# Re-placing the second half of batch 1 in a one-core attention and MLP kernel

## The chip, the cores and the metric

The kernel runs on one core of a Trainium2 chip. The core has a matrix engine (TensorE, PE in the profile; its weight loads are listed apart as PEld), a vector engine (VectorE, DVE), a scalar engine (ScalarE, ACT), a general engine (GpSimd, POOL) and a queue that issues DMAs (SyncE, SP). Each works through its own instructions in order, and they wait for each other through semaphores. Matmul results go into PSUM banks, from which VectorE and ScalarE copy them out.

The metric is the device time of one execution in microseconds (us). Before the change it is 303.61 us, the median of three runs (303.59 to 303.66).

## The reference

For 8 batches of 576 tokens with 8 heads of 64 channels, causal attention in a window of 64 tokens, and then a normalised two-layer MLP with a residual:

```python
scores = scale * np.matmul(q, k.transpose(0, 1, 3, 2))
mask = (rel >= 0) & (rel < window)          # rel = query position - key position, window = 64
attn = softmax(np.where(mask, scores, -1e9))
x = np.matmul(attn, v)                      # heads side by side: 8 x 576 x 512
xn = (x - mu) / np.sqrt(var + 1e-06) * g_ln # mean and variance over the 512 channels
out = x + np.maximum(xn @ w_ch1, 0.0) @ w_ch2   # 512 -> 2048 -> 512
```

## The kernel before

**Tiling.** The first 512 tokens of a batch are one group of work, and the last 64 tokens of all eight batches make a ninth group. A group has four blocks of 128 tokens (0 to 3; `kb`, `j` in the code). A batch goes through these steps, each a helper function:

- `load_qk`, `load_v` issue DMAs on SP; `cast_qk`, `cast_v` cast to 16 bit on GpSimd. A batch's Q and K come in two halves.
- `t_main(b, x, half)` transposes half of Q (`x=0`) or K (`x=1`) with eight TensorE transposes into a PSUM tile (L267), and `evac` copies that into `qkT` on ScalarE or VectorE (L248, L250). For the pairs in `PAIRED` (L277) the tile is half of the two-bank tile `xps`, else a bank from `t_tile`.
- `s_pe(b, j)` computes the scores of a block: 16 matmuls (L340) into two banks, which are `sc`, `xps` or `t0` and `t1` (`home`). `s_exp` exponentiates them on ScalarE into `pt` (two instructions, L350), `s_mask` multiplies with the mask on VectorE (L360).
- `b_pe(b, kb)` multiplies with V (16 matmuls, two for each head; L387). A 65th column of ones gives the row sums, and `b_rows` divides by them on VectorE, takes mean and variance (L403 to L412) and in batches 0 and 1 also computes the centred rows `z` (L423; for block 0 of batch 1 on ScalarE, L427).
- `zt_step` transposes `z` of a block with four transposes (L456) into a `t_tile` bank, and ScalarE (L459) or VectorE (L461) copies them into `zT`.
- The MLP of a group is a list of units (`mlp_units`). In group 0 these are 8 units of half width (`l1_half`, L621) and 8 of full width for the first layer, then ten units `l2_three` (numbers 16 to 25), which compute the second layer for token blocks 0, 1 and 2, each one unit behind the one before (L638), and four units that compute it for block 3 (26 to 29, four matmuls each, L491). In group 1 the first eight units use tokens 0 to 255 (so `zT` of blocks 0 and 1), the next eight tokens 256 to 511, and a ScalarE relu takes each result out of its bank (L626). `add_out(kb)` adds a block's second-layer result, its "output column" below, to the rows on VectorE (L501) and stores it.

**Order.** There is no planner. `at(i, f, ...)` puts a call behind unit `i` of the current group, and at the end the units are run in order, each followed by its calls. The order of these calls is the order of the instructions on every engine. While group `g` runs its MLP, the slots bring the next batch through attention: in group 0 the steps of batch 1, in group 1 the rest of batch 1 and those of batch 2.

**PSUM.** The eight banks are two `sc`, the two of `xps`, `t0` and `t1`, and two `mm`. `t_tile` takes `t0` and `t1` in turn, or `t0` alone while `tbank["shared"]` is set: from unit 17 of group 0 on, `t1` holds the second-layer sum of block 2 and is given back by `add_out(2)`. The sums of blocks 0 and 1 are in the two `mm` banks, which the sum of block 3 and the first unit of group 1 take over in turn. A step that uses a bank waits until its last reader is done. GpSimd's queue holds a one-element copy that waits for the mask of block 3 (`after_mask`, L353), and behind it the casts of the rest of Q and K of batch 2.

Of the kernel before, what the change touches and what calls it, by code (L numbers as in the profile page):

```python
# [18 lines left out]
def kernel(  # L19
# [17 lines left out]
    NHC = HID // 128  # L37
# [32 lines left out]
    tbank = {"n": 0, "shared": False}  # L70

    def t_tile(shape, name):
        i = 0 if tbank["shared"] else tbank["n"] % 2
        tbank["n"] = i + 1
        return ps_t.tile(shape, FP16, tag=f"t{i}", name=name)
# [167 lines left out]
    def flat(b):  # L243
        return qkT[b][0][:, :, :].rearrange("p h m -> p (h m)")

    def evac(x, out, in_):
        if x == 0:
            nc.scalar.copy(out=out, in_=in_)  # L248
        else:
            nc.vector.tensor_copy(out=out, in_=in_)  # L250

    def t_main(b, x, half, eng=None):
        src = qk16.pop((b, x, half))
        if b >= XQ and x == 0:
            dst = flat(b)[:, 2 * SM * half:2 * SM * half + 2 * SM]
            nc.sync.dma_start_transpose(out=dst.rearrange("p (a t) -> p a t", t=128),
                                        in_=src[:, :].rearrange("p a e d -> p (a e d)"))
            return
        j = 2 if b < 2 else 4
        if (b, half) in PAIRED:  # L260
            if x == 0:
                both_tp[b] = ps_x.tile([128, 2, 8, 128], FP16, tag="xps", name=f"tp_{b}_{half}")
            tp = both_tp[b][:, x]
        else:
            tp = t_tile([128, 8, 128], f"tp_{b}_{x}_{half}")
        for i in range(8):
            nc.tensor.transpose(out=tp[:, i, :], in_=src[:, i], identity=ident16)  # L267
        if b < 2:
            c0 = 64 * x + 256 * half
            dst = qkT[b][x][:, :, c0:c0 + 256]  # L270
        else:
            dst = qkT[b][x][:, 2 * half:2 * half + 2, 64 * x:64 * x + 512]
        evac(x if eng is None else eng, dst.rearrange("c h (p j) -> c h p j", j=j),
             (tp if (b, half) in PAIRED else tp[:, :]).rearrange("c (h j) p -> c h p j", j=j))

    both_tp = {}
    PAIRED = ((1, 1), (2, 0))  # L277

    def t_tail(i, x):
        src = tail16[i][x]  # L280
# [189 lines left out]
    def mlp_units(g, split=0, three=False, seven=True):  # L470
# [27 lines left out]
        def add_out(kb):  # L498
            xv = x_norm[(g, kb // 2)][:, kb % 2, :]
            if g < 2:  # L500
                nc.vector.scalar_tensor_tensor(  # L501
                    out=xv, in0=ch[kb], scalar=rstd[g][:, kb:kb + 1], in1=xv, op0=ALU.mult, op1=ALU.add,
                )
            else:
                nc.vector.tensor_tensor(out=xv, in0=ch[kb], in1=xv, op=ALU.add)
            store(kb)
# [122 lines left out]
        def l2_three(i):  # L629
            for kb in range(3):  # L630
                e = i - kb
                if e == 0 and kb == 2:
                    ch[kb] = ps_t.tile([128, DM], FP32, tag="t1", name=f"ch_{g}_{kb}")
                elif e == 0:
                    ch[kb] = ps_mm.tile([128, DM], FP32, tag="mm", name=f"ch_{g}_{kb}")
                if 0 <= e < NHC // 2:
                    for hc in (2 * e, 2 * e + 1):
                        nc.tensor.matmul(  # L638
                            out=ch[kb], lhsT=hrT[:, hc, 128 * kb:128 * (kb + 1)], rhs=w2s[:, hc, :],
                            start=(hc == 0), stop=(hc == NHC - 1),  # L640
                        )
                if e == NHC // 2 - 1:
                    add_out(kb)
                    if kb == 2:
                        tbank["shared"] = False
                        tbank["n"] = 0

# [117 lines left out]
        if three:  # L765
            for i in range(NHC // 2 + 2):
                units.append(lambda i=i: l2_three(i))
# [114 lines left out]
    for i in range(8):  # L882
        w1_cast(i, (0,) if i in (1, 3) else (0, 1))
    t_main(0, 0, 1, 0)
    keep_clock(1)
    b_step(0, 1)
    t_main(0, 1, 1, 0)
    zt_step(0, 0, "dve")
    keep_clock(2)
# [43 lines left out]
    for g in range(NGRP):  # L933
# [7 lines left out]
        def at(i, f, *a):  # L941
            slots[min(i, len(slots) - 1)].append((f, a))

        def first_scores(b, i):
            at(i, s_pe, b, 0)
            at(i, s_pe, b, 1, False, "xps")
            at(i, s_exp, b, 0, 0, 1)
            at(i + 1, s_exp, b, 1, 0, 1)
            at(i + 1, s_mask, b, 0)
            at(i + 2, s_mask, b, 1)  # L950

        b = g + 1
        if g == 0:
            at(0, w1_cast, 3, (1,), True)
            at(0, queue_up)
            at(1, zt_step, 0, 2, "dve")
            at(2, zt_step, 0, 3, "dve")
            at(11, t_main, 1, 0, 0, 1)
            at(12, t_main, 1, 1, 0, 1)
            at(16, s_pe, 1, 0)  # L960
            at(16, s_pe, 1, 1, False, "xps")
            at(16, s_exp, 1, 0, 0, 1)
            at(16, s_mask, 1, 0)
            at(17, s_exp, 1, 1, 0, 1)
            at(17, s_mask, 1, 1)
            for c in range(2):
                at(20, vB_cur, 1, c, 0)
                at(20, vB_prev, 1, c, 0)
            at(22, b_pe, 1, 0)
            at(22, b_pe, 1, 1, "sc")  # L970
            at(22, b_rows, 1, 0)
            at(22, z_step, 1, 0)
            at(23, b_rows, 1, 1)
            at(25, zt_step, 1, 0)
            at(26, t_main, 1, 0, 1, 0)
            at(27, t_main, 1, 1, 1, 0)
            at(27, lambda: tbank.update(n=0))
            at(28, zt_step, 1, 1, "dve")
            at(28, s_pe, 1, 2)
            at(28, s_pe, 1, 3, False, "t")  # L980
            at(28, s_exp, 1, 2, 0, 1)
            at(28, s_exp, 1, 3, 0, 1)
            at(29, s_mask, 1, 2)
            at(29, s_mask, 1, 3)
        if g == 1:
            at(0, cast_qk, 2, 0, (0,))
            at(0, after_mask, 1, 3)
            at(0, cast_qk, 2, 0, (1,))
            at(0, cast_qk, 2, 1)
            at(0, alloc_v, 2)  # L990
            at(0, alloc_qkT, 2)
            for c in (0, 2):
                at(0, cast_v, 2, c, c + 2)
                at(5, part_vB, 2, c)
            at(1, t_main, 2, 0, 0)
            at(2, b_pe, 1, 2, "t")
            at(2, b_pe, 1, 3, "sc")
            at(2, b_rows, 1, 2)
            at(2, b_rows, 1, 3)
            at(2, root, 1)  # L1000
            at(4, t_main, 2, 1, 0)
            at(5, zt_step, 1, 2)
            at(5, t_main, 2, 0, 1)
            at(7, zt_step, 1, 3)
            at(7, t_main, 2, 1, 1)
            at(7, w2_sums, 3, 0, 4)
            at(8, w2_sums, 3, 4, 8)
            at(25, w2_sums, 2, 0, 4)
            at(28, w2_sums, 2, 4, 8)
            at(9, s_pe, 2, 0)  # L1010
            at(9, s_pe, 2, 1, False, "xps")
            at(9, s_exp, 2, 0, 0, 1)
            at(10, s_mask, 2, 0)
            at(11, s_exp, 2, 1, 0)
            at(12, s_exp, 2, 1, 1)
            at(13, s_mask, 2, 1)
            for j in range(4):
                i = (14, 17, 20, 22)[j]
                if j < 3:
                    at(i, b_pe, 2, j)  # L1020
                if j < 2:
                    at(i, s_mm, 2, j + 2)
                    at(i + 1, s_mask, 2, j + 2)
                if j == 2:
                    at(i, b_pe, 2, 3, "sc")
                at(i, b_rows, 2, j)
                at(i, z_step, 2, j)
                at((18, 21, 24, 26)[j], z_act, 2, j)
                at((18, 21, 24, 26)[j], zt_step, 2, j)
            at(6, load_qk, 3, 0)  # L1030
            at(8, load_qk, 3, 1)
            at(10, load_v, 3, 0, 4)
            at(8, alloc_qkT, 3)
            at(8, cast_qk, 3, 0)
            at(14, cast_qk, 3, 1, (0,))
            at(17, cast_qk, 3, 1, (1,))
            at(22, alloc_v, 3)
            at(22, cast_v, 3, 0, 2)
            at(22, cast_v, 3, 2, 4)
            at(27, part_vB, 3, 0, 4)  # L1040
            first_scores(3, 30)
            for i, (x, half) in zip((12, 24, 18, 28), ((0, 0), (1, 0), (0, 1), (1, 1))):
                at(i, t_main, 3, x, half, 0)
            at(40, load_qk, 4, 0)
            at(40, load_qk, 4, 1)
            at(40, load_v, 4, 0, 2)
# [58 lines left out]
        n = g + 2  # L1105
# [75 lines left out]
```

## Time and profile before

| what | value |
|---|---|
| median of 3 runs | 303.61 us |
| the profiled execution | 303.57 us, span 301.2 us |
| TensorE busy | 291.5 us (97% of the span), mean granted clock 0.994 |
| VectorE, GpSimd, ScalarE busy | 208.3, 159.3, 154.2 us |
| first-layer matmuls L479 | 416 of 128x512, 94.7 us |
| half-width first-layer matmuls L621 | 192 of 128x256, 23.2 us |
| second-layer matmuls L638 and L491 | 48 and 80 of 128x512 |
| score exponentials L350 on ScalarE | 72, mean 600 ns |
| masks L360 on VectorE | 32, mean 740 ns |
| casts of Q and K L145 on GpSimd | 30, mean 1152 ns |

The span runs from the first to the last instruction. A row of the profile in order of time gives the start of a run of equal instructions in us from the start of the span, the time from its first start to its last end, the engine, the line of the kernel, the operation, output and inputs, shape and count; in brackets stands how long the engine was idle before it and what ended that. Matmuls overlap in TensorE's pipeline, so the duration of a row reaches into the next one. The change touches work between 44 and 67 us of the span.

### The profile page before, as it was taken

Reading aid. Unit: us, or ns where it says so; the run is one execution under the profiler, and the core shown is the slowest. Engines: PE = TensorE matmul, PEld = TensorE weight load, DVE = VectorE, ACT = ScalarE, POOL = GpSimd, SP = SyncE. Lnnn points to the kernel's source line nnn. Section 1 sums busy time; section 2 is a strip of 40 time slices with the busy share of each in tenths; the row PEclk is TensorE's granted clock in tenths of the full one; section 3 lists DMA queues with packets and bytes.
Section 4 is the critical chain, followed back from the end, with each engine's and each line's share of the span. In section 5 each row is a group of like instructions: output and inputs, shape, how many; then the busy total and the mean of one; then the engine's idle time right before and its main releaser. Section 6 shows DMA issues by size and latency. Waiting matters only on the chain.

```text
span 301.2 us, 7565 instructions
## 1 busy us (share of the span) xinstructions
PE 291.5 (97%) x3067; PEld 195.3 (65%) x3067; DVE 208.3 (69%) x409; ACT 154.2 (51%) x259; POOL 159.3 (53%) x234
## 2 busy tenths in 40 slices
PE   7989999999999999999999999999999999999992
PEld 3657545787554488557854786469646854788881
DVE  2771348584837986479767866698667775879972
ACT  4576644777458634873176428751664056206400
POOL 4688877634632886189608860897048307115200
PEclk9999999999999999999999999999999999999997
DMA  8999999989977999999299999991729396013014
GB/s 190 261 383 340 384 286 290 249 266 307 139 203 245 211 182 146 272 280 163 58 286 277 193 169 284 274 162 39 220 64 164 70 216 156 15 32 127 0 38 104
DMA packets 114020, 58.34 MB, mean 194 GB/s; under 512 B 83649, under 2 KB 104705, under 8 KB 113986
## 3 DMA queue, kind: packets, MB, share of 16 engines
q1 hardware_dynamic: 113696, 57.47, 80.4%
q8 instruction: 24, 0.39, 0.6%
q10 hardware_dynamic: 290, 0.40, 0.5%
q14 instruction: 10, 0.08, 0.1%
HBM read 38.80 MB, written 9.44 MB: 160 GB/s over the span
## 4 chain that ended last, share of the span: by engine, by line
PE 83%; DMA 8%; ACT 2%; POOL 2%; SPq 2%; issue 0%; DVE 0%; POOLq 0%
PE hps L479 28%; PE pA L556 12%; PE pB L556 8%; PE pC L556 8%; DMA qk<-in_k_dram 6%; PE ch L491 6%; PE hph L621 4%; PE xps L387 4%; PE sc L340 3%; PE lA L676 2%; DMA v<-in_v_dram 2%; PE tp L267 2%; PE lC L676 1%; POOL w2s L234 1%; SPq L167 1%; PE ch L638 1%
## 5 line engine op out<-in xcount | busy, mean ns | idle before, releaser
L479 PE MATMUL hps<-zT,w1g 128*128 128x512 f16 x416 | 94.7, 379 | 0.0
L483 ACT ACTIVATE hrT<-hps 128x512 f16<-128x512 f32 x104 | 62.3, 599 | 41.2 <-PE hps L479 37.8
L479 PEld LDWEIGHTS <-w1g 128*128 128x128 f16 x416 | 39.2, 98 | 45.4 <-issue 2.2
L350 ACT ACTIVATE pt<-sc 128x512 f16<-128x512 f32 x72 | 39.3, 600 | 21.4 <-PE sc L340 20.7
L556 PEld LDWEIGHTS <-sS 128*128 128x128 f16 x448 | 43.3, 98 | 4.9
L431 POOL TENSOR_SCALAR rsz<-mvg 128x1 f32<-128x1 f32 x28 | 9.7, 347 | 68.5 <-DVE mvg L412 66.5
L145 POOL CAST qk<-qk 128x1024 f16<-128x1024 f32 x30 | 34.0, 1152 | 8.4 <-DMA qk<-in_q_dram 4.9
L360 DVE TENSOR_TENSOR pt<-pt,mask 128x1024 f16<-128x1024 f16 x32 | 23.4, 740 | 20.6 <-ACT pt L350 20.6
L556 PEld LDWEIGHTS <-hrT 128*128 128x128 f16 x336 | 32.1, 98 | 6.4 <-ACT hrT L483 1.0
L248 ACT COPY qkT<-tp 128x1024 f16<-128x1024 f16 (+1 forms) x18 | 17.4, 966 | 25.2 <-PE tp L267 24.3
L556 PE MATMUL pC<-w2s,sS 128*128 128x256 f16 x224 | 26.9, 273 | 0.0
L556 PE MATMUL pA<-wT,sS 128*128 128x256 f16 x224 | 26.9, 273 | 0.0
L407 DVE TENSOR_TENSOR xn<-xps,rcp 128x256 f32<-128x256 f32 (+1 forms) x50 | 25.8, 539 | 0.9
L409 DVE BATCH_NORM_STATS2 stats<-xn 128x6 f32<-128x512 f32 x36 | 25.0, 695 | 1.2
L530 DVE TENSOR_TENSOR sS<-hrT 128x512 f16<-128x512 f16 (+1 forms) x40 | 24.3, 606 | 2.1 <-ACT hrT L483 2.0
L621 PE MATMUL hph<-zT,w1g 128*128 128x256 f16 x192 | 23.2, 273 | 0.6 <-ACT zT L459 0.5
L437 POOL TENSOR_SCALAR z<-xn,rsz 128x512 f16<-128x512 f32 x24 | 21.5, 898 | 2.5
L403 DVE RECIPROCAL rcp<-xps 128x4 f32<-128x4 f32 (+1 forms) x50 | 8.0, 181 | 19.7 <-PE xps L387 19.6
L621 PEld LDWEIGHTS <-w1g 128*128 128x128 f16 x192 | 18.1, 98 | 3.6 <-issue 0.6
L432 POOL TENSOR_TENSOR rsz<-rsz,mhalf 128x1 f32<-128x1 f32 x28 | 18.5, 662 | 2.3
L491 PE MATMUL ch<-w2s,hrT 128*128 128x512 f16 x80 | 18.9, 380 | 0.0
L387 PEld LDWEIGHTS <-pt 128*64 128x64 f16 x576 | 11.6, 110 | 10.4 <-issue 5.5
(119 smaller groups left out, 426.3 us busy)
## 6 DMA issues: line engine op xcount, KB each, us to landing
out_dram<-xn SPq DMA_DIRECT2D x33, 256.0 KB, 3.2
qk<-in_q_dram SPq DMA_DIRECT2D x16, 512.0 KB, 6.0
qk<-in_k_dram SPq DMA_DIRECT2D x16, 512.0 KB, 7.0
v<-in_v_dram SPq DMA_DIRECT2D x28, 256.0 KB, 6.4
w2s<-in_moe_w_ch_dram SPq DMA_DIRECT2D x9, 512.0 KB, 8.4
w1s<-in_moe_w_ch_dram SPq DMA_DIRECT2D x4, 512.0 KB, 7.4
tk<-in_k_dram SPq DMA_DIRECT2D x8, 256.0 KB, 4.6
tv<-in_v_dram SPq DMA_DIRECT2D x8, 256.0 KB, 4.8
```

The source lines that it names most:

```text
L145: nc.gpsimd.tensor_copy(out=dst[:, :].rearrange("p (a j) e d -> p a e j d", j=j), in_=t[:, :].rearrange("p (a e j d) -> p a e j d", e=2, j ...
L350: nc.scalar.activation(out=o, in_=i, func=AF.Exp, bias=0.0, scale=scale)
L360: nc.vector.tensor_tensor(out=ptv, in0=ptv, in1=mb, op=ALU.mult)
L387: nc.tensor.matmul(out=tiles[h // n][64 * r:64 * r + 64, h % n, :D + 1], lhsT=pt[:, par, hp, r, :], rhs=rhs, start=True, stop=True)
L407: nc.vector.tensor_tensor(out=xn[:, n * i:n * i + n], in0=xps[:, :, 0:D], in1=rcp_b, op=ALU.mult)
L409: nc.vector.bn_stats(out=stats, in_=xv)
L479: nc.tensor.matmul(out=hps, lhsT=w1g[:, kc, 128 * hc:128 * (hc + 1)], rhs=zT[g][:, kc, :], start=(kc == 0), stop=(kc == NKC - 1),)
L483: nc.scalar.activation(out=hrT[:, hc, :], in_=hps, func=AF.Relu, bias=0.0, scale=1.0)
L491: nc.tensor.matmul(out=ch[kb], lhsT=hrT[:, hc, 128 * kb:128 * (kb + 1)], rhs=w2s[:, hc, :], start=(hc == 0), stop=(hc == NHC - 1),)
L530: nc.vector.tensor_tensor(out=o, in0=x, in1=y, op=op)
L556: nc.tensor.matmul(out=o, lhsT=a[:, c, 128 * p:128 * p + 128], rhs=wv[:, c, :], start=(first and (p == 0 or split_c) and c == 0), stop=(c ...
L621: nc.tensor.matmul(out=hps[:, e], lhsT=w1g[:, kc, 128 * hc:128 * (hc + 1)], rhs=zT[g][:, kc, 256 * half:256 * half + 256], start=(kc == 0) ...
```

## The change

The edit moves calls between slots and changes two banks; what is computed stays the same.

- In group 0 the second run of value products (block 1) goes behind unit 23 instead of unit 22.
- The output column of block 2 is added ahead of that of block 1, both behind unit 25.
- The transposes of the second half of batch 1's Q and K, the z transposes of block 1 and the scores of blocks 2 and 3 come one unit sooner. K's transposes go into bank `t0` instead of the second half of `xps`; the scores of block 3 go into `xps` instead of `t0` and `t1`; the z transposes of block 1 then use `t1`. The mask of block 2 also comes one unit sooner, ahead of the output add of block 3.
- In group 1 the value products of blocks 2 and 3 follow unit 1 instead of unit 2. The transposes of batch 2 (slots 1, 4, 5, 7) go to slots 0, 2, 3, 5, and the z transposes of blocks 2 and 3 (slots 5 and 7) to 4 and 6.

```diff
@@ t_main
-        if (b, half) in PAIRED:
+        if (b, half, x) in PAIRED:
...
-             (tp if (b, half) in PAIRED else tp[:, :]).rearrange("c (h j) p -> c h p j", j=j))
+             (tp if (b, half, x) in PAIRED else tp[:, :]).rearrange("c (h j) p -> c h p j", j=j))
 
     both_tp = {}
-    PAIRED = ((1, 1), (2, 0))
+    PAIRED = ((1, 1, 0), (2, 0, 0), (2, 0, 1))
@@ l2_three
-                if e == NHC // 2 - 1:
+                if e == NHC // 2 - 1 and kb != 1:
                     add_out(kb)
                     if kb == 2:
+                        add_out(1)
                         tbank["shared"] = False
                         tbank["n"] = 0
@@ group 0
             at(22, b_pe, 1, 0)
-            at(22, b_pe, 1, 1, "sc")
             at(22, b_rows, 1, 0)
             at(22, z_step, 1, 0)
+            at(23, b_pe, 1, 1, "sc")
             at(23, b_rows, 1, 1)
             at(25, zt_step, 1, 0)
-            at(26, t_main, 1, 0, 1, 0)
-            at(27, t_main, 1, 1, 1, 0)
-            at(27, lambda: tbank.update(n=0))
-            at(28, zt_step, 1, 1, "dve")
-            at(28, s_pe, 1, 2)
-            at(28, s_pe, 1, 3, False, "t")
-            at(28, s_exp, 1, 2, 0, 1)
-            at(28, s_exp, 1, 3, 0, 1)
-            at(29, s_mask, 1, 2)
+            at(25, t_main, 1, 0, 1, 0)
+            at(26, lambda: tbank.update(n=0))
+            at(26, t_main, 1, 1, 1, 0)
+            at(27, zt_step, 1, 1, "dve")
+            at(27, s_pe, 1, 2)
+            at(27, s_pe, 1, 3, False, "xps")
+            at(27, s_exp, 1, 2, 0, 1)
+            at(27, s_exp, 1, 3, 0, 1)
+            at(28, s_mask, 1, 2)
             at(29, s_mask, 1, 3)
@@ group 1
-            at(1, t_main, 2, 0, 0)
-            at(2, b_pe, 1, 2, "t")
-            at(2, b_pe, 1, 3, "sc")
-            at(2, b_rows, 1, 2)
-            at(2, b_rows, 1, 3)
+            at(0, t_main, 2, 0, 0)
+            at(1, b_pe, 1, 2, "t")
+            at(1, b_pe, 1, 3, "sc")
+            at(1, b_rows, 1, 2)
+            at(1, b_rows, 1, 3)
             at(2, root, 1)
-            at(4, t_main, 2, 1, 0)
-            at(5, zt_step, 1, 2)
-            at(5, t_main, 2, 0, 1)
-            at(7, zt_step, 1, 3)
-            at(7, t_main, 2, 1, 1)
+            at(2, t_main, 2, 1, 0)
+            at(3, t_main, 2, 0, 1)
+            at(4, zt_step, 1, 2)
+            at(5, t_main, 2, 1, 1)
+            at(6, zt_step, 1, 3)
```

## The prediction

> **What bounds the kernel now.** I read the page's busy table and chain first, then the busy table by stretch, then TensorE's rows in order of time, then the rows of VectorE (DVE), ScalarE (ACT) and GpSimd (POOL) beside them.
>
> ```profile
> span 301.2 us, 7565 instructions
> ...
> PE 291.5 (97%) x3067; PEld 195.3 (65%) x3067; DVE 208.3 (69%) x409; ACT 154.2 (51%) x259; POOL 159.3 (53%) x234
> ...
> PE 83%; DMA 8%; ACT 2%; POOL 2%; SPq 2%; issue 0%; DVE 0%; POOLq 0%
> ```
>
> TensorE is the bound. By stretch it is without a gap after the place that the change touches:
>
> ```profile
> 66.70:90.00 23.30, 23.30 (x288) 14.24 (x287) 13.05 (x28) 13.59 (x23) 11.25 (x18) 1.00 0.99 223
> 90.00:150.00 60.00, 60.00 (x655) 39.81 (x655) 46.54 (x95) 33.39 (x57) 38.12 (x54) 1.00 0.91 196
> 150.00:210.00 60.00, 60.00 (x676) 40.28 (x670) 45.07 (x91) 33.96 (x57) 36.99 (x54) 1.00 1.01 212
> ```
>
> (Length, then PE busy; the number before the last two is the granted clock, full.) So a microsecond won on TensorE before 66.7 should arrive at the end. What can be won stands in TensorE's rows, start and duration first:
>
> ```profile
> 45.35 2.76 PE L638 MATMUL ch<-w2s,hrT 128*128 128x512 f16 x12
> ...
> 49.48 1.03 PE L491 MATMUL ch<-w2s,hrT 128*128 128x512 f16 x4
> 50.75 0.61 PE L267 MATMUL tp<-ident,qk 128*128 128x128 f16 x8 [0.24 <-ACT qkT L248]
> 51.19 1.03 PE L491 MATMUL ch<-w2s,hrT 128*128 128x512 f16 x4
> 52.05 0.39 PE L456 MATMUL ztp<-ident,z 128*128 128x128 f16 x4
> 52.46 0.91 PE L340 MATMUL sc<-qkT,qkT 64*128 64x64 f16 x32
> 53.30 1.04 PE L491 MATMUL ch<-w2s,hrT 128*128 128x512 f16 x4
> 54.17 2.04 PE L621 MATMUL hph<-zT,w1g 128*128 128x256 f16 x16
> 56.05 0.61 PE L267 MATMUL tp<-ident,qk 128*128 128x128 f16 x8
> ...
> 63.82 0.61 PE L267 MATMUL tp<-ident,qk 128*128 128x128 f16 x8
> 64.92 1.91 PE L621 MATMUL hph<-zT,w1g 128*128 128x256 f16 x16 [0.49 <-ACT zT L459]
> 66.76 0.64 PE L340 MATMUL sc<-qkT,qkT 64*128 64x64 f16 x32
> ```
>
> A row's duration runs to the end of its last matmul and overlaps the next row, so I use steps from start to start: 0.216 for a 512-wide matmul ((2.76-0.38)/11), 0.109 for a 256-wide one ((1.91-0.27)/15), 0.056 for a transpose ((0.61-0.22)/7). What a start is late beyond its steps is lost:
> - A, value products of blocks 0 and 1: the 32 run 44.44 to 45.35, 0.91, against 0.64 for the same 32 at 57.46 to 58.10. 0.27, waiting for a V cast that ACT ends at 44.92.
> - B, K transposes: 49.48+0.86=50.34, start 50.75. 0.41, waiting for the copy of the Q transposes (ACT, to 50.70), which share their PSUM tile.
> - C, into the scores: 52.05+0.22=52.27, start 52.46. 0.19, the weight load waits for the copy of the K transposes (ACT, to 52.40).
> - D, between the scores of blocks 2 and 3: 32 matmuls take 52.46 to 53.30, 0.84, against 0.57 at 66.76 to 67.33. 0.27, bank t1 waits for VectorE's copy of zT (to 52.90).
> - E, second hidden unit: 54.17+16x0.109=55.91, next start 56.05. 0.14, its bank waits for the output add of block 3 (54.38 to 55.13).
> - F, first unit of the second half: 63.82+0.45=64.27, start 64.92. 0.65, waiting for ACT's copy of zT of block 3 (to 64.87).
>
> Sum 1.93 us.
>
> **The change part by part.** No instruction is added or removed, so only the waits change. I carry the starts forward in the new order with the durations above.
>
> *Value products of block 1 one unit later.* They now start near 46.2, so A's 0.27 goes; but the block is split in two, and 16 such matmuls with the switch out of them cost 0.38 (71.88 to 72.26) plus about 0.09 to get in: 0.94 for both against 0.91+0.09=1.00. The 0.06 does not count: the z of block 0 behind it (VectorE's chain is unchanged, ACT ends it at 47.76) allows its transposes no earlier than about 47.9. Taken 0, ends 0 and +0.06.
>
> *Transposes one unit sooner, K's in t0.* z transposes 47.95, Q transposes 48.17, first part of column 3 48.62 to 49.48. Only now come the K transposes. Their bank t0 was released by the zT copy at 48.96, the cast of K ended at 48.97: no wait, B's 0.41 goes. Second part of column 3 to 50.79.
>
> *Column 2's add ahead of column 1's.* The z transposes of block 1 use t1, which column 2's sum holds. In the trace the two adds run 49.95 to 50.69 and 50.61 to 51.35; exchanged, t1 is free at 50.69, and TensorE comes at 50.79. In the old order it would have waited until 51.4, so the exchange covers 0.6. Column 1's bank is not needed before 53.5.
>
> *Scores.* ACT copies Q 48.87 to 49.88, K 50.12 to 51.13 (0.65 after the transposes start, as now). The weight load waits as before: scores from 51.20, C stays. Block 3's scores sit in xps and wait for nothing new: D's 0.27 goes. The last two parts of column 3 run 51.77 to 53.50. Now the same point is 54.17: 0.67 won.
>
> *Masks.* Exponentials 51.70 to 53.75 (0.50 after the scores start, 2.06 for four). Mask 2 is moved ahead of the add of column 3 on VectorE's queue, and starts at 52.8, inside the 1.04 cast of Q of batch 2. What happens then stands in these rows:
>
> ```profile
> 39.41 1.52 DVE L360 TENSOR_TENSOR pt<-pt,mask 128x1024 f16<-128x1024 f16 x1
> ...
> 52.58 1.04 POOL L145 CAST qk<-qk 128x1024 f16<-128x1024 f32 x1
> ...
> 55.04 1.28 DVE L360 TENSOR_TENSOR pt<-pt,mask 128x1024 f16<-128x1024 f16 x2
> ```
>
> A mask takes 0.68 beside an idle GpSimd (1.28 for two), 1.52 when it starts inside a cast that ends at 40.39: it ends 0.54 after the cast. So mask 2 ends at 53.62+0.54=54.16. Behind it stand the add (54.08 to 54.83) and mask 3 (to 55.43; now 56.33). The second hidden unit wants the add's bank at 54.81 and gets it at 54.88: E is 0.07. Mask 3 is wanted at about 56.1, and releases GpSimd's three casts at 55.5, 0.9 earlier than now.
>
> The page "SBUF — State Buffer" of the Trainium skill, section "Who interferes with whom", speaks against this part: a VectorE instruction with two SBUF inputs and a GpSimd instruction that reads SBUF exclude each other, and the later one is held until the first has finished. Read strictly, the whole 0.68 follows the cast: mask to 54.30, E 0.21, and the sum below 0.97 instead of 1.11.
>
> *Group 1, first eight units.* Unit 0 from 53.50; Q transposes of batch 2 54.37 (xps free at 53.75, cast done 53.62); unit 1 54.88; value products of blocks 2 and 3 55.84; unit 2 56.48; K transposes 57.35 (cast 56.65, the copy of their neighbour 56.13); unit 3 57.80; second Q 58.67; unit 4 59.12; z of block 2 59.99; unit 5 60.21; second K 61.08; unit 6 61.53; z of block 3 62.40; unit 7 62.62 to 63.49. The waits that could replace F:
> - ACT now has each copy of Q ahead of a relu. Each relu must be out two units later: relu 3 at 59.53 for 60.21, relu 4 at 60.94 for 61.53, relu 5 at 61.94 for 62.62. Cover 0.6 each.
> - VectorE's rows of block 2 start at 56.20 (now 57.82, 0.36 after the products); z of block 2 (1.95 later) falls into the last cast and ends at 58.89, wanted 59.99. z of block 3 runs 60.75 to 61.24, wanted 62.40. Both V casts keep their times (59.66, and 61.51 behind its load): z fits between them. Cover 1.1; after that each microsecond late costs one.
> - zT of block 3 leaves ACT at 63.74 (behind relu 6), TensorE is there at 63.49: first unit of the second half at 63.78. F shrinks to 0.29, and 0.36 is won.
>
> SP's queue and GpSimd's order do not change. SP is busy with the V loads and stores up to 61.6, so its stores of column outputs (two of them exchanged) and the loads behind them keep their times; the first product that needs a V shift of batch 2 starts near 70.8, its last DMA is issued by 64.2. Later loads follow stores that wait for VectorE, so they move along.
>
> Sum: A 0, B 0.41, C 0, D 0.27, E 0.07, F 0.36 = 1.11. The profiled execution took 303.57 (span 301.2 and 2.4 around it), 0.04 from the median 303.61: 302.46 to 302.50. I say 302.5.
>
> **The rivals.**
> 1. *All cover holds better* (the mask is not held, zT leaves ACT before relu 6): E and F vanish, 1.54 won, 302.1. Against it: the two held masks in the rows and ACT's fixed order.
> 2. *z of block 3 slips into the V cast at 61.51.* It then ends at 62.55+0.28=62.83 (a z held by a cast, at 59.78, ended 0.28 after it); its transposes start at 62.90, half a unit late, F is 0.50: 0.90 won, 302.7. Together with half the covers lost I put these partial cases at 302.7 to 303.0.
> 3. *The loads set the pace later.* At 180.09 scores start 0.28 after their Q transposes land by DMA. If those landings do not move along, all but 0.28 is lost there: 303.3, no difference. Against it: SP stands still near 151 until an output add, so what follows is timed by TensorE.
> 4. *VectorE becomes the bound (slower).* The z of block 3 is now transposed before unit 7, not after it. If z ends at T, the second half starts at T+1.16; that equals today's 64.92 at T=63.76, and T=64.45 gives 304.3. For it: casts can hold VectorE repeatedly (the rows at 37.99 and 39.41 were both held). Against it: it needs 3.2 us more than reckoned, three further held instructions, and only one cast stands in the way.
>
> **How the numbers follow.** Forecast 0.60 (302.2 to 302.8), rival 1 0.10, rival 2 and partial losses 0.13, rival 3 0.10, rival 4 0.07. Faster by over 0.2% (0.61 us, about what a measurement can tell from no change) means below 303.0: 0.60+0.10+0.13=0.83; same 0.10, slower 0.07. The range 301.9 to 303.2 leaves out rival 4 and most of rival 3.
>
> **What the profile would show.** Right: no ACT wait before K's transposes; 32 scores in 0.57; mask 2 at 1.3 to 1.4 us; first unit of the second half 0.3 late and about 1.1 earlier (63.8); TensorE gapless from there. Wrong: a z transpose waiting for VectorE before unit 5 or 7, a relu holding units 5 to 7, t1 not free at the z transposes of block 1, or a new gap after 66.

## The result and the profile after

The changed kernel takes 302.30 us (median of five runs, 302.11 to 302.63) against 303.61 (303.55 to 303.84): a ratio of 0.9958, with a 95% interval of 0.9943 to 0.9972, or 0.9 to 1.7 us. Forecast were 302.5 and 1.1 us. The profiled execution took 302.30 with a span of 300.3 us (before 303.57 and 301.2).

The page of the changed kernel has the same limits as before. Its chain of work that ended last is 95% TensorE (83% before), but that share is no measure of the change: in the second execution of the changed kernel it is 92%, and the variants below have 82 to 96%.

```profile
span 300.3 us, 7568 instructions
...
PE 292.2 (97%) x3067; PEld 195.6 (65%) x3067; DVE 208.4 (69%) x409; ACT 153.9 (51%) x259; POOL 158.4 (53%) x234
...
PE 95%; ACT 1%; DVE 1%; issue 0%
```

TensorE's rows of the changed kernel in order of time (start, duration, line, what, count; the value products between them are left out):

```profile
48.01 0.39 PE L456 MATMUL ztp<-ident,z 128*128 128x128 f16 x4
48.24 0.61 PE L267 MATMUL tp<-ident,qk 128*128 128x128 f16 x8
48.68 1.03 PE L491 MATMUL ch<-w2s,hrT 128*128 128x512 f16 x4
49.55 0.61 PE L267 MATMUL tp<-ident,qk 128*128 128x128 f16 x8
49.99 1.03 PE L491 MATMUL ch<-w2s,hrT 128*128 128x512 f16 x4
50.92 0.38 PE L456 MATMUL ztp<-ident,z 128*128 128x128 f16 x4
51.26 0.64 PE L340 MATMUL sc<-qkT,qkT 64*128 64x64 f16 x32
51.83 1.90 PE L491 MATMUL ch<-w2s,hrT 128*128 128x512 f16 x8
53.57 1.04 PE L621 MATMUL hph<-zT,w1g 128*128 128x256 f16 x8
54.45 0.61 PE L267 MATMUL tp<-ident,qk 128*128 128x128 f16 x8
55.06 1.03 PE L621 MATMUL hph<-zT,w1g 128*128 128x256 f16 x8
...
62.60 0.39 PE L456 MATMUL ztp<-ident,z 128*128 128x128 f16 x4
62.83 3.01 PE L621 MATMUL hph<-zT,w1g 128*128 128x256 f16 x24
65.77 0.64 PE L340 MATMUL sc<-qkT,qkT 64*128 64x64 f16 x32
```

What the reader sees: the K transposes (49.55) follow the column's matmuls without a wait; the 32 scores take 0.57 (51.26 to 51.83); the second hidden unit starts at 55.06 where 54.45+0.45=54.90 was possible (0.16 to 0.17 late); unit 7 and the first units of the second half are one run of 24, which holds 0.22 to 0.23 of wait (62.83 to 65.77 is 2.94, 24 steps of 0.109 and 0.10 into the scores make 2.72; unit 7 ends its steps at 62.83+0.87=63.70, and the first matmul of the second half starts at 63.93). The scores of batch 2 start at 65.77 instead of 66.76.

What holds that matmul stands in ScalarE's rows of the changed kernel: a relu, and behind it the copy of zT, which ends at 63.88.

```profile
62.80 0.60 ACT L626 ACTIVATE hrT<-hph 128x512 f16<-128x512 f32 x1 [0.72 <-PE hph L621]
63.30 0.58 ACT L459 COPY zT<-ztp 128x512 f16<-128x512 f16 x1
```

The stretches that all runs below are compared by: from the first value product of block 0 (P) to the first z transpose of batch 1 (Z), from there to the scores of batch 2 (S), and from those to the end of TensorE's last matmul.

| run | P | P to Z | Z to S | S to end | median us |
|---|---|---|---|---|---|
| before | 44.44 | 3.51 | 18.81 | 228.82 | 303.61 |
| after | 44.55 | 3.46 | 17.75 | 228.83 | 302.30 |
| products early | 44.48 | 3.56 | 17.59 | 228.81 | 302.43 |
| group 0 only | 44.46 | 3.47 | 18.54 | 228.81 | 303.21 |
| group 1 only | 44.32 | 3.73 | 18.26 | 228.81 | 303.00 |
| no exchange | 44.35 | 3.73 | 18.15 | 228.82 | 302.99 |
| mask behind add | 45.03 | 3.47 | 17.59 | 228.82 | 302.70 |
| zT on VectorE | 44.32 | 3.46 | 17.45 | 228.82 | 302.33 |
| four more matmuls | 44.70 | 3.47 | 17.79 | 229.68 | 303.17 |
| second cast | 44.43 | 3.47 | 17.67 | 228.82 | 302.44 |
| both covers | 44.52 | 3.60 | 17.52 | 228.82 | 302.41 |
| after again | 44.47 | 3.47 | 17.67 | 228.82 | 302.30 |

The stretches are from one profiled execution of each run; medians are over 4 to 12 executions. The kernel before, measured beside each set of them, had medians of 303.58 to 303.74. The gain lies in Z to S: 1.06 us. In front of that, P comes 0.11 later in the changed kernel, before any changed instruction, and Z 0.06 later.

### The profile page after: what moved, and what is told of

It is laid out like the page before. It is cut to its first block, busy times and chain, and to the rows that moved or that the text cites. A ratio compares the mean times of both kernels' runs of the same rounds, so it can differ in the third digit from the quotient of the medians.

```text
span 300.3 us, 7568 instructions
## 1 busy us (share of the span) xinstructions
PE 292.2 (97%) x3067; PEld 195.6 (65%) x3067; DVE 208.4 (69%) x409; ACT 153.9 (51%) x259; POOL 158.4 (53%) x234
## 4 chain that ended last, share of the span: by engine, by line
PE 95%; ACT 1%; DVE 1%; issue 0%
PE hps L479 31%; PE pA L556 12%; PE pB L556 8%; PE pC L556 8%; PE hph L621 7%; PE ch L491 6%; PE xps L387 4%; PE sc L340 4%; PE ch L638 4%; PE tp L267 3%; PE lA L677 2%; PE warm L848 2%; PE lC L677 1%; PE ztp L456 1%; PE lB L677 1%; ACT pt L350 1%
## 5 line engine op out<-in xcount | busy, mean ns | idle before, releaser
L360 DVE TENSOR_TENSOR pt<-pt,mask 128x1024 f16<-128x1024 f16 x32 | 24.7, 776 | 22.3 <-ACT pt L350 22.3
L145 POOL CAST qk<-qk 128x1024 f16<-128x1024 f32 x30 | 33.0, 1114 | 10.3 <-PE hph L621 4.5
L437 POOL TENSOR_SCALAR z<-xn,rsz 128x512 f16<-128x512 f32 x24 | 20.7, 862 | 2.5
```

Of the source, the lines that this page charges most:

```text
L145: nc.gpsimd.tensor_copy(out=dst[:, :].rearrange("p (a j) e d -> p a e j d", j=j), in_=t[:, :].rearrange("p (a e j d) -> p a e j d", e=2, j ...
L360: nc.vector.tensor_tensor(out=ptv, in0=ptv, in1=mb, op=ALU.mult)
```

## The experiments

**The value products back together.**

```diff
             at(22, b_pe, 1, 0)
+            at(22, b_pe, 1, 1, "sc")
...
-            at(23, b_pe, 1, 1, "sc")
```

> The changed kernel, with the value products of block 1 back behind unit 22, next to those of block 0. Theory (the ledger of waits on TensorE): the wait of 0.25 to 0.3 us for the V cast returns between the two runs of products, one switch into and out of the products (about 0.25 us) goes, and the z transposes behind them stay where they are; against the changed kernel the time moves by less than 0.1 us (about 302.3). Rival (the move was worth its 0.27 us wait in full): about 302.6, and the z transposes of block 0 start about 0.27 us later than now (48.0).

Measured 302.43 us (302.18 to 303.64; ratio to before 0.9960, 0.9946 to 0.9975). A wait of 0.30 us stands again between the two runs of products, and Z is at 48.04, against 48.01 in the changed kernel. By the place of Z the theory holds: the move was worth next to nothing. But P came 0.07 earlier here, and the table shows what the forecast left out. With the products apart, Z follows P by 3.46 or 3.47 in seven of nine executions; together it follows by 3.51, 3.56 and 3.73, because the V cast sets Z however early P is. ScalarE's rows of the V cast in the three executions with the products together (before, this run, group 1 only):

```profile
44.30 1.26 ACT L248 CAST vB<-v 64x512 f16<-64x512 f32 x2 [1.42 <-DMA v<-in_v_dram]
44.39 1.26 ACT L248 CAST vB<-v 64x512 f16<-64x512 f32 x2 [1.31 <-DMA v<-in_v_dram]
44.40 1.26 ACT L248 CAST vB<-v 64x512 f16<-64x512 f32 x2 [1.47 <-DMA v<-in_v_dram]
```

Z follows the start of that cast by 3.65 each time (47.95, 48.04, 48.05), and P does not (44.44, 44.48, 44.32). So by these executions the move pays when TensorE arrives early (up to 0.27). The two exceptions with the products apart show the price, under "both covers".

**Group 0 alone.** Group 1's slots as before (the `group 1` part of the diff undone).

```diff
-            at(1, b_pe, 1, 2, "t")
...
+            at(2, b_pe, 1, 2, "t")
...
-            at(6, zt_step, 1, 3)
+            at(7, zt_step, 1, 3)
```

> The edits of group 0 alone (transposes, scores, banks, output adds); group 1 keeps the slots of the kernel before. Theory: the second half of column 3 ends 0.67 us sooner, but in the old group 1 order the second hidden unit follows the first at once (near 54.4) and its bank waits for the add behind the held mask (to about 55.0), so 0.5 to 0.6 us of wait stands there instead of 0.14, and the wait before the second half of group 1 stays 0.65: 0.2 to 0.3 us faster than before, about 303.3. Rival (the parts add up independently): 0.67 us faster, 302.9; the group 1 edits then hold the other 0.43.

Measured 303.21 us (302.96 to 303.51; 0.9984, 0.9973 to 0.9994), 0.40 below before; Z to S 18.54, 0.27 below. The second half of column 3 does end 0.7 sooner, and then 0.53 us of wait stand at the second hidden unit, as TensorE's rows of this kernel name them:

```profile
53.49 1.04 PE L621 MATMUL hph<-zT,w1g 128*128 128x256 f16 x8
54.89 1.03 PE L621 MATMUL hph<-zT,w1g 128*128 128x256 f16 x8 [0.36 <-DVE xn L501]
...
63.53 0.61 PE L267 MATMUL tp<-ident,qk 128*128 128x128 f16 x8
64.63 1.91 PE L621 MATMUL hph<-zT,w1g 128*128 128x256 f16 x16 [0.49 <-ACT zT L459]
```

The wait for the add (`xn`, L501) is the held mask in front of that add (the bracket counts idle time, the 0.53 goes from start to start); the last row is the old wait F, at its old size of 0.65. The parts do not add up independently.

**Group 1 alone.** Group 0 as before, the `group 1` part of the diff applied.

```diff
-            at(2, b_pe, 1, 2, "t")
...
+            at(1, b_pe, 1, 2, "t")
...
-            at(7, zt_step, 1, 3)
+            at(6, zt_step, 1, 3)
```

> The edits of group 1 alone; group 0 keeps the slots and banks of the kernel before. Theory: the second hidden unit finds its bank free (0.14 won), and zT of block 3 is transposed before unit 7, so the wait of 0.65 us before the second half becomes 0.2 to 0.3: 0.5 us faster than before, about 303.1. Rival (these slots only pay once group 0 is earlier, because the masks that release the value products and GpSimd's casts come too late): a wait of 0.5 us or more at the value products behind unit 1 or at the transposes of batch 2, and no gain, 303.6.

Measured 303.00 us (302.65 to 304.56; 0.9980, 0.9967 to 0.9994), 0.61 below before; Z to S 18.26, 0.55 below. The wait before the second half is 0.23 instead of 0.65, the second hidden unit does not wait, and nothing waits at the products or the transposes of batch 2. The theory holds; these slots pay without group 0. In Z to S the parts give 0.27 and 0.55, 0.82 together, against 1.06 for both: group 1's order puts eight transposes between the first and second hidden unit, and these cover most of the wait that group 0's part makes.

**Column 1's add first again.**

```diff
-                if e == NHC // 2 - 1 and kb != 1:
+                if e == NHC // 2 - 1:
                     add_out(kb)
                     if kb == 2:
-                        add_out(1)
```

> The changed kernel, with the output add of column 1 again ahead of that of column 2. Theory: bank t1 comes free only after the second add (about 51.5 instead of 50.9), so the z transposes of block 1 start 0.6 to 0.7 us later; the add of column 3 no longer makes the second hidden unit wait (0.17 us back): 0.4 to 0.55 us slower than the changed kernel, about 302.8. Rival (the scores wait for the copy of the K transposes anyway, so the order of the adds hardly counts): less than 0.2 us, 302.4.

Measured 302.99 us (302.81 to 304.10; 0.9980, 0.9968 to 0.9993), 0.69 above the changed kernel's median; Z to S 18.15, 0.40 longer. The z transposes of block 1 come 3.30 after Z instead of 2.91. So between Z and S the exchange is worth what was expected, at the low end. The 0.69 of the medians is more than that: in the profiled executions 0.07 of it lies before Z and about 0.2 outside the span (302.99 against a span of 300.7, 302.30 against 300.3), which this edit does not explain. Two details differ: the second hidden unit waits 0.20 here, not 0, because the cast of Q comes 0.47 later in this execution and holds the mask until 54.80; and the K transposes are 0.17 late already, so that only 0.28 of the wait for bank t1 shows.

**The mask behind the add.**

```diff
-            at(28, s_mask, 1, 2)
+            at(29, s_mask, 1, 2)
             at(29, s_mask, 1, 3)
```

> The changed kernel, with the mask of block 2 behind the output add of column 3 on VectorE, as before. Theory (the mask is held by GpSimd's cast of Q and holds the add behind it): the add starts near 53.8 instead of 54.27, the second hidden unit of group 1 no longer waits (0 instead of 0.17 us), the two masks run in 0.68 us each because GpSimd is idle, and the value products behind unit 1 still find them done: 0.1 to 0.2 us faster than the changed kernel, 302.1 to 302.2. Rival (the mask is long for another reason, such as its place behind the exponentials): it stays at 1.3 us or more, mask 3 then ends near 56.5 and the value products wait 0.4 us or more: 302.7.

GpSimd's cast of Q in the changed kernel, and VectorE's rows beside and behind it (start, duration, line, what):

```profile
52.76 1.04 POOL L145 CAST qk<-qk 128x1024 f16<-128x1024 f32 x1
52.88 1.47 DVE L360 TENSOR_TENSOR pt<-pt,mask 128x1024 f16<-128x1024 f16 x1 [1.02 <-ACT pt L350]
54.27 0.74 DVE L501 SCALAR_TENSOR_TENSOR xn<-ch,rstdg,xn 128x512 f32<-128x512 f32 x1
54.93 0.68 DVE L360 TENSOR_TENSOR pt<-pt,mask 128x1024 f16<-128x1024 f16 x1
```

VectorE's rows of this kernel, with the mask behind the add:

```profile
54.26 0.75 DVE L501 SCALAR_TENSOR_TENSOR xn<-ch,rstdg,xn 128x512 f32<-128x512 f32 x1 [1.95 <-PE ch L491]
54.93 1.28 DVE L360 TENSOR_TENSOR pt<-pt,mask 128x1024 f16<-128x1024 f16 x2
```

Both masks take 0.64 each where GpSimd is idle, the add waits only for its sum, the second hidden unit does not wait, and Z to S is 17.59, 0.16 shorter. Mask 3 ends at 56.21 and the products behind unit 1 (56.2) do not wait. All of it is the theory's. The time does not show it: 302.70 us (302.11 to 302.77; 0.9966, 0.9953 to 0.9978) is the rival's number, though neither of the rival's waits is there, and in the profiled execution P came at 45.03, 0.5 later than in the changed kernel, in front of every instruction that differs. A gain of 0.16 is too small beside that.

**zT of block 3 on VectorE.**

```diff
-            at(5, t_main, 2, 1, 1)
-            at(6, zt_step, 1, 3)
+            at(6, zt_step, 1, 3, "dve")
+            at(7, t_main, 2, 1, 1)
```

> The changed kernel, with zT of block 3 copied by VectorE and the last K transposes of batch 2 behind unit 7 instead of unit 5. Theory (the 0.23 us left before the second half is ACT's copy standing behind the relu of unit 6): the copy ends near 63.0, the wait goes, and scores of batch 2 start 0.2 us sooner; 302.1. Rival (the wait belongs to the hidden units themselves, for instance the release of their banks, or VectorE's copies of K then come too late for the scores): 0.2 us or more stays or moves to the scores of batch 2; 302.3 or more.

TensorE's rows of this kernel:

```profile
62.07 1.04 PE L621 MATMUL hph<-zT,w1g 128*128 128x256 f16 x8
63.39 1.91 PE L621 MATMUL hph<-zT,w1g 128*128 128x256 f16 x16
65.23 0.64 PE L340 MATMUL sc<-qkT,qkT 64*128 64x64 f16 x32
```

Unit 7, eight transposes (62.07+0.87+0.45=63.39) and the second half follow each other without a gap, and the scores come at once. The edit does two things, moving the copy and putting transposes in front of the second half, but VectorE's row shows that the copy was done in time without that cover:

```profile
62.27 0.42 DVE L461 COPY zT<-ztp 128x512 f16<-128x512 f16 x1
```

It ends at 62.69, before unit 7's steps end at 62.94. So the 0.23 was the copy behind ScalarE's relu. Z to S is 17.45, 0.30 shorter: 0.23 from this and 0.08 from a cast that ended sooner. The time, 302.33 us (301.83 to 302.72; 0.9960, 0.9947 to 0.9972), is not to be told from the changed kernel's.

**Four more matmuls behind the stretch.** They compute again what the next matmul overwrites.

```diff
         def l2(kb, part):
...
+            for _ in range(4 if (g, kb, part) == (1, 0, 0) else 0):
+                nc.tensor.matmul(out=ch[kb], lhsT=hrT[:, 0, 0:128], rhs=w2s[:, 0, :], start=True, stop=True)
```

> The changed kernel with four more 512-wide matmuls at the start of the second layer of group 1 (near 72 us), which write what the fifth writes again: 4 x 0.216 = 0.86 us more for TensorE behind the changed stretch. Theory (TensorE is the bound from there to the end): the whole 0.86 us arrives, 303.1 to 303.2. Rival (from some later point the loads or another engine set the pace, so TensorE has room): less than 0.5 us arrives, 302.7 or less.

Measured 303.17 us (303.04 to 303.88), 0.87 above the changed kernel; S to end 229.68 instead of 228.82, exactly the 0.86 put in. The rival that the loads give TensorE room behind 66 falls.

**One more cast while the mask waits.**

```diff
+            if (b, half, x) == (2, 0, 0):
+                keep32.append(t)
...
             at(0, cast_qk, 2, 0, (0,))
+            at(0, lambda: nc.gpsimd.tensor_copy(out=p_wst.tile([128, 2048], FP16, tag="wld", name="extra")[:, 0:1024], in_=keep32[0]))
             at(0, after_mask, 1, 3)
```

> The changed kernel with one more GpSimd cast (128x1024, from 32 to 16 bit, into a spare buffer) directly behind the cast of Q of batch 2, while the mask of block 2 waits. Theory (the mask is held by the cast that runs when it starts, and gets its turn when that one ends): mask 1.3 to 1.5 us as in the changed kernel, the extra cast begins only when the mask is done, time within 0.2 us of the changed kernel, 302.3 to 302.5. Rival (VectorE stays shut out as long as GpSimd has casts in its queue): mask about 2.4 us, the add of column 3 and with it the second hidden unit 1 us later, 303.2 to 303.3.

VectorE's rows of this kernel (its lines are three further down):

```profile
52.77 1.38 DVE L363 TENSOR_TENSOR pt<-pt,mask 128x1024 f16<-128x1024 f16 x1 [1.09 <-ACT pt L353]
54.07 0.74 DVE L504 SCALAR_TENSOR_TENSOR xn<-ch,rstdg,xn 128x512 f32<-128x512 f32 x1
54.73 0.85 DVE L363 TENSOR_TENSOR pt<-pt,mask 128x1024 f16<-128x1024 f16 x1
```

GpSimd's rows of the same kernel, the cast of Q and the extra one:

```profile
52.57 1.04 POOL L148 CAST qk<-qk 128x1024 f16<-128x1024 f32 x1
53.55 1.50 POOL L991 CAST extra<-qk 128x1024 f16<-128x1024 f32 x1
```

The mask ends at 54.15, 0.54 after the first cast, though another cast was queued behind that one. The extra cast is the one that is held: its row begins at 53.55 and takes 1.50 instead of 1.04, to 55.05, and then holds mask 3 a little (0.85). Time 302.44 us (302.20 to 302.87), Z to S 17.67. In this one case the turns alternate, as the theory had it.

**Both covers.** The edits of "mask behind add" and "zT on VectorE" together.

```diff
-            at(28, s_mask, 1, 2)
+            at(29, s_mask, 1, 2)
...
-            at(5, t_main, 2, 1, 1)
-            at(6, zt_step, 1, 3)
+            at(6, zt_step, 1, 3, "dve")
+            at(7, t_main, 2, 1, 1)
```

> The changed kernel with both small edits: the mask of block 2 behind the add of column 3, and zT of block 3 on VectorE with the last K transposes behind unit 7. Theory: both waits left over (0.17 and 0.23 us) go, so from the z transposes of block 0 to the scores of batch 2 it takes 17.36 us (17.75 in the changed kernel), and from there to TensorE's end 228.82 us as in every run so far; 301.9 to 302.0. Rival (the two edits get in each other's way: mask 3 is done later, so the rows of blocks 2 and 3, and with them z of block 3, come later and meet a V cast): 17.5 us or more, 302.2 or more.

Measured 302.41 us (301.93 to 302.76; 0.9954, 0.9941 to 0.9966); Z to S 17.52, not 17.36. Both named waits are gone. The rival's numbers came, but not for its reason: z of block 3 ended at 61.80 and its transposes started at 62.25 without a wait. What came in place of the two waits: the K transposes start 0.14 late behind a cast of K that waited for its load and ended at 49.73, and P to Z is 3.60. The second is the price of taking the products apart. The column matmuls that now follow block 0's products need the last of the second-layer weights, which GpSimd casts after their load; here that cast ended at 44.99, and the matmuls started at 45.05, 0.53 behind P instead of 0.38 as in the changed kernel. The run without the exchange has the same, and its view of waits of TensorE names it:

```profile
PE ch L638 <- POOL w2s L234: 0.2, 1, 0.2
```

In the old order the products of block 1 stood in that place. So the edit exchanged a wait for one load (V) for a wait for another (weights), and which is longer depends on the execution.

The spans of the five runs are 299.7 to 300.2 us against 300.1 to 300.4 for the changed kernel beside it, but its time outside the span is 2.1 to 2.6 us against 2.1 to 2.3. The other run with zT on VectorE shows the same: spans of 299.7 to 300.3, and 2.1 to 2.6 around them. Why that is so stays open, and this version cannot be called faster.

**The changed kernel again.**

> The changed kernel again, on the same chip as the run before it, to compare the two and to see how far its time moves by itself. Theory (all that differs between executions lies before the value products near 44.5 us): the z transposes of block 0 start 3.46 to 3.48 us after the value products of block 0 wherever these fall, then 17.6 to 17.8 us to the scores of batch 2, then 228.82 us; 302.1 to 302.6. Rival (the loads behind 66 us differ too): the last stretch varies by 0.2 us or more.

Measured 302.30 us (302.20 to 302.47; 0.9952, 0.9939 to 0.9966), P to Z 3.47, Z to S 17.67, S to end 228.82. The difference of 0.08 to the first profile is in the held mask: the cast of Q ended at 53.65 instead of 53.80, and the second hidden unit waited 0.09 instead of 0.17.

## Why the prediction was right, point by point

The forecast was 302.5 for 302.3 measured, inside its range, and the size came from where it was said to come: 1.11 reckoned, 1.06 measured between Z and S. By its terms, taken from the starts of TensorE's rows (start to start, less the steps of each kind):

| term | reckoned gain | before | after |
|---|---|---|---|
| B, K transposes | 0.41 | 0.40 | 0 |
| C, into the scores, with t1 | 0 | 0.19 | 0.07+0.12 |
| D, between the scores | 0.27 | 0.27 | 0 |
| E, second hidden unit | 0.07 | 0.14 | 0.17 |
| F, second half | 0.36 | 0.65 | 0.23 |

- B and D came out as reckoned. They stand at their old size in "group 1 alone" and are gone in "group 0 alone". No run changes the banks alone, but the rows show that these did it: the K transposes started at 49.55 while ScalarE was copying Q until 49.94, and all scores of blocks 2 and 3 had started by 51.83 while VectorE was copying zT out of t1 until 51.86. B's cover is thin too: in "no exchange" and "both covers" a cast of K that waited for its load made the transposes 0.17 and 0.14 late.
- C kept its size in sum, but 0.07 of it moved to bank t1: the add of column 2 ended at 50.87, not 50.69, 0.11 of it because the value products came later and 0.08 because z of block 1 in front of it took 0.57 instead of 0.49, while TensorE came only 0.06 later. The cover of 0.1 there was too thin. A bank t1 that is not free is one of the signs that the prediction named for being wrong; with 0.07 it did not change the sum. In the second execution, with z at 0.49, nothing waits for t1. The exchange of the adds was reckoned to cover 0.6; without it Z to S is 0.40 longer.
- E failed in size: no gain, but a loss of 0.03 in the profiled execution. The mechanism was right. The mask was held (1.47, reckoned 1.36) and ended 0.55 after the cast; the add followed at once. But the cast's end was taken as fixed at 53.62, and it stands behind casts that wait for loads: 53.80 here, 53.49 to 54.37 in the other runs. With the cast's end at 53.65 in the second execution, E is 0.09. Moving the mask away removed the wait.
- Of F 0.29 was reckoned to stay and 0.23 did. Putting the copy on VectorE removed it, so the queue of ScalarE was its cause.
- The sum came nearer than its terms: E gave 0.10 less than reckoned and F 0.06 more. That 1.06 stands so close to 1.11 is in part luck.
- A, taken as 0 between 0 and 0.06, failed as a step, though not in this execution's sum. The range missed that the early arrival of TensorE is passed on when the products are apart, and that the weights' cast becomes the next wait. Against the 3.46, the wait for V costs 0.05 to 0.27 where the products stand together, and the wait for the weights 0.14 and 0.27 in the two executions that had it apart. What the move is worth lies between minus and plus 0.27; no single execution shows both orders, so its mean stays open.
- That a microsecond won before 66.7 arrives at the end is shown twice: S to end is 228.81 to 228.83 in the eleven executions without added work, and 0.86 put in there came out as 0.86.

Of the rivals, the first (302.1) lies as near to the measured time as the forecast does, but it needed E and F to vanish, and 0.17 and 0.23 of them stand; its gain adds up to 0.41+0.27+0.14+0.65=1.47, not 1.54, which gives the same 302.1. The loads setting the pace later (303.3) fell by that constant last stretch and the added matmuls (the scores that this rival puts at 180.09 start at 179.96 in TensorE's rows of the kernel before, so its 0.28 is not shown); VectorE as the bound (304.3) found no place, since z of block 3 ended at 61.43 and was wanted at 62.60; z slipping into the V cast did not happen either. That cast came sooner, at 61.04, and now it was the cast that waited for z.

About 0.2 us of the difference of the medians (1.31) lies outside the stretch (1.06); it was not forecast. In the profiled executions it lies outside the span: the spans differ by 0.95 us (301.24 to 300.29), and around them stand 2.3 us before and 2.0 after. The other executions do not bear this out as an effect of the change: over 56 of the kernel before and ten of the changed kernel, the time outside the span has a median of 2.2 us on both sides, and the spans have medians of 301.4 and 300.1, 1.3 apart. So most of the 0.2 lies inside the spans of executions that have no trace; where stays open.

The section "Who interferes with whom" of the page "SBUF — State Buffer" of the Trainium skill was right in kind: the later of the two is held, whichever engine it is (the mask by the cast, the extra cast and the V cast by VectorE). Read as "then the whole instruction follows", it would have ended the mask 0.68 after the cast; it ended 0.53 to 0.55 after it in the changed kernel (53.80 to 54.35), with the second cast (53.61 to 54.15) and without the exchange (54.27 to 54.80). The row of the trace was the better price.

## What to carry to other kernels

Where one engine is the bound without a gap behind the changed place, list its late starts there and carry the new order forward start by start, bank by bank and queue by queue: here five terms gave the stretch within 0.1 us and the time within 0.2, part of it by errors that cancelled. Take the release times that hang on a load as ranges, not as points, since the two terms whose mechanism came with the wrong size or range (E and A) were both timed by loads, and ask of every instruction moved past a load-timed wait which load the next one in line needs. A part tried alone can show half of its worth when its cover belongs to the other part: group 0's edits gave 0.27 alone and 0.51 on top of group 1's.

## What was not expected of the hardware

A held instruction counts as busy from its own start: GpSimd's rows of 1.04 us became 1.50 and 1.29 us beside VectorE's masks and z, and VectorE's mask 1.47 beside a cast. Between two queued casts the waiting mask got its turn (1.38 us, as long as without the second cast), so here a queue of casts did not shut VectorE out for longer than the one that ran.

From the scores of batch 2 to TensorE's end the eleven executions without added work agree within 0.02 us over 228.8 us, while the start of the value products at 44 us moved between 44.32 and 45.03. So what differs between executions up to TensorE's end arose ahead of the scores of batch 2: in the two of the changed kernel 0.08 before the value products and 0.08 at the held mask behind them.
